# Cosine attention and an MLP mixer on one core: w1 fetched early, the copies of w2 spread over three slot ends, and two pieces of the start moved to GpSimd

## Chip, core and metric

One core of a Trainium2 chip. The metric is the device time of the program in microseconds (us), median of several runs. The kernel before takes 393.95 us. All runs whose state is recorded were in the fast state; the mean clock granted to the tensor engine differs from run to run (0.985 to 1.0).

## The reference, cut to what matters

```python
# q, k, v: (8 batches, 12 heads, 448 rows, 64), float32
q_n = q / (norm(q) + 1e-6);  k_n = k / (norm(k) + 1e-6)
attn = softmax(q_n @ k_n.T / tau)
x = (attn @ v) in the shape (8, 448, 768)
u = x + (relu(x.T @ w_tok1) @ w_tok2).T      # token mixing
out = u + relu(u @ w_ch1) @ w_ch2            # channel mixing
```

## The kernel before

The kernel works on 48 pairs of heads, one pair in each "slot" of a software pipeline. The 448 rows of a head are 3 x 128 "main" rows and 64 "X" rows. For each pair: squares and sums of q and k, their norms, scaled q and k, a transpose, scores, exponentials, and the product with v; then token mixing (w1 is w_tok1, w2 is w_tok2) two or three slots later and, from slot 6 on, channel mixing, which fills the tensor engine. In these traces every engine runs its instructions in the order in which the program gives them. So an instruction that waits holds back all that stand behind it on its engine: in the changed kernel the sums of pair 2 wait 2.66 us for GpSimd, and the copy behind them waits as long; a run below puts that copy ahead of the sums, and it comes sooner.

The start, before slot 0, and the ends of the first slots are what the change touches:

```python
    def weights_tok():
        nc.gpsimd.dma_start(out=w1t[:, 0:NC, :], ...)       # main part of w1
        nc.gpsimd.dma_start(out=w1t[0:XR, NC, :], ...)      # its X rows
        nc.gpsimd.dma_start(out=w2n[0][:], ...)             # w2, still in its natural order

    def place_w2():                                         # w2 into the order that the matmul reads
        nc.vector.tensor_copy(out=w2t[:, :, XR:S]..., in_=w2n[0][:, :, 0:SM]...)
        nc.vector.tensor_copy(out=w2t[:, :, S:S + XR], in_=w2n[0][:, :, SM:S])

    def place_w2_odd():                                     # the X columns once more, for odd batches
        nc.vector.tensor_copy(out=w2t[:, :, 0:XR], in_=w2n[0][:, :, SM:S])
    # ...
        squares_x(0, nc.scalar, nc.gpsimd)
        rnorms(0, 21, 33)
        scaled(1, nc.gpsimd)
        # ...
        score_main0(0, 2)
        squares(2, nc.scalar, nc.gpsimd)
        score_main0(1)
        scaled_x(0, nc.vector, 0, 1)          # pair 0's X rows
        scaled_x(0, nc.gpsimd, 1, HP)         # those of pairs 1 and 2
        sums(2)                               # vector engine
        score_main0(2)
        tpose_x(0, pst)
        for lo, n in ((P * NC, P), (P * 7, XR)):
            nc.vector.tensor_copy(out=qks[0][:, lo:lo + n], in_=pst[:, lo:lo + n])
        rnorms(0, 33, 45)
        score_rest0()
        score_x(0)
        weights_tok()
        cast_vx(0)
        cast_v(0)                             # vector engine
        scaled(2, nc.gpsimd)
        for i in range(NP_ALL + 2):           # the slots
            # ... pair 3's squares in slot 0, q and k both on the scalar engine
            if i == 2:
                place_w2()
            if i == 3:
                place_w2_odd()
```

Of the kernel before, what the change touches and what calls it, by code (L numbers as in the profile page):

```python
# [22 lines left out]
def kernel(  # L23
# [12 lines left out]
    nc = tc.nc  # L36

    B, H, S, E = q.shape
# [5 lines left out]
    NC = 3  # L44
# [45 lines left out]
    w2n = []  # L90
# [46 lines left out]
    def mh(at, p):  # L137
        return at[p // HP][:, 2 * (p % HP):2 * (p % HP) + 2]

    def weights_tok():  # L140
        nc.gpsimd.dma_start(out=w1t[:, 0:NC, :], in_=moe_w_tok1[0:SM].rearrange("(p c) t -> p c t", c=NC))
        nc.gpsimd.dma_start(out=w1t[0:XR, NC, :], in_=moe_w_tok1[SM:S])
        w2n.append(mix.tile([P, TT, S], FP16, name="w2n", tag="gt16", bufs=1))
        nc.gpsimd.dma_start(out=w2n[0][:], in_=moe_w_tok2.rearrange("(tt p) s -> p tt s", p=P))

    def place_w2():
        nc.vector.tensor_copy(out=w2t[:, :, XR:S].rearrange("t a (c p) -> t a c p", c=NC),
                              in_=w2n[0][:, :, 0:SM].rearrange("t a (p c) -> t a c p", c=NC))
        nc.vector.tensor_copy(out=w2t[:, :, S:S + XR], in_=w2n[0][:, :, SM:S])  # L149

    def place_w2_odd():
        nc.vector.tensor_copy(out=w2t[:, :, 0:XR], in_=w2n[0][:, :, SM:S])

    def weights_ch1(i):
        n = C // 2
# [31 lines left out]
    def squares_x(n, eq, ek):  # L187
        square(eq, sqx[0:XR, 0:6], xh(xq, n, 6))
        square(ek, sqx[:, 6:9], xh(xk, n, HP))
# [257 lines left out]
    def at(slots):  # L447
        got = {}
        for p, s in slots.items():
            got.setdefault(s, []).append(p)  # L450
        return got


    FIRST = NPAIR
    early_sq = {3: 0, 4: 1, 5: 1, 6: 3, 7: 4, 8: 5, 9: 5, 10: 6, 11: 7, 12: 8, 13: 9, 14: 9, 15: 10, 16: 11, 17: 11}
    sq_slot = {p: early_sq.get(p, p - 6) for p in range(3, NP_ALL)}
    sq_at = at(sq_slot)
    sum_at = at({p: s + 1 for p, s in sq_slot.items() if p < 8 or p >= 18})

    rn_at = {}  # L460
    for n in range(1, NHALF):
        for c0, c1 in ((0, 21), (21, 45)) if n < 4 else ((0, 45),):
            s = 1 + sq_slot[3 * n + (0 if c1 == 21 else 2)]
            rn_at.setdefault(s, []).append((n, c0, c1))
    sc_at = at({p: {7: 6}.get(p, p - 2 if p < DMA_FROM else p - 3) for p in range(3, NP_ALL)})
    early_qk = {2: 0, 3: 4, 4: 6, 5: 7}
# [30 lines left out]
    def norm_begin(p, eq, ek):  # L497
        squares(p, eq, ek)
        if p % HP == 0:
            squares_x(p // HP, eq, ek)  # L500
# [11 lines left out]
    with tc.manual_schedule():  # L512
# [53 lines left out]
        tpose_main(0, pst, 0)  # L566
        tpose_main(0, pst, 1)
        squares_x(0, nc.scalar, nc.gpsimd)
        rnorms(0, 21, 33)
        scaled(1, nc.gpsimd)  # L570
        nc.scalar.copy(out=qks[0][:, 0:SM], in_=pst[:, 0:SM])
# [1 line left out]
        nc.vector.tensor_copy(out=qks[0][:, 512:512 + SM], in_=pst[:, 512:512 + SM])  # L573
        rnorms(0, 0, 9)
        busy(w, 2)
        score_main0(0, 2)
        squares(2, nc.scalar, nc.gpsimd)
        score_main0(1)
        scaled_x(0, nc.vector, 0, 1)
        scaled_x(0, nc.gpsimd, 1, HP)  # L580
        sums(2)
        score_main0(2)
# [3 lines left out]
        rnorms(0, 33, 45)  # L586
        score_rest0()
        score_x(0)
        weights_tok()
        cast_vx(0)  # L590
        cast_v(0)
        scaled(2, nc.gpsimd)
        for i in range(NP_ALL + 2):
            if i < DMA_FROM:
                loads(i)
            if DMA_FROM <= i + 2 < NP_ALL:
                dma_tpose(i + 2)
            if i - 2 in X_DMA:
                x_tpose(i - 2)
            for p in ut_at.get(i, ()):  # L600
                u_tpose(p)
            if i >= DMA_FROM:
                loads(i)

            left = next((t + 1 - i for t in sorted(tok2_at) if t >= i + (i == FIRST) and
                         any(p % NPAIR == NPAIR - 1 for p in tok2_at[t])), 6)
            if FIRST <= i < 2 * NPAIR:
                quota = max(len(queue) - 6, 0) * ns(S, DT) / (2 * NPAIR - i)
            else:
                quota = max(sum(t for t, _ in queue) - 2000.0, 0.0) / left  # L610
            def next_qk(p):
                if p < min(DMA_FROM, NP_ALL):
                    qk_copy(p, tpose(p))

            def tok2(p):
                m_tok2(p)
                if p % NPAIR == NPAIR - 1:
                    queue.extend(ch_units(p // NPAIR))

            def norm_rn():  # L620
                for n, c0, c1 in rn_at.get(i, ()):
                    rnorms(n, c0, c1)

            def next_sq(ps):
                for p in ps:
                    norm_begin(p, nc.scalar if p < 18 else nc.gpsimd, nc.scalar if p == 3 else nc.vector if p in (10, 11, 12, 15) else nc.gpsimd)

            if i == FIRST:
                next_sq([9])
                rnorms(2, 21, 33)  # L630
                norm_scale(7, nc.gpsimd)
                pv(i - 1)
                m_tok1(i - 2)
                tok2(i - 3)
                next_qk(i)
                tok2(i - 2)
                m_tok1(i - 1)
                score(i, 0)
                score(i, 1)
                score(i, 2)  # L640
                tok2(i - 1)
                norm_sums(8)
                norm_sums(9)
            elif 0 < i < NP_ALL:
                score(i, 0, 2 if i < 4 else 0)
                score(i, 1)
                score(i, 2)
            for p in sum_at.get(i, ()):
                norm_sums(p)
            if i < FIRST:  # L650
                norm_rn()

            if i < FIRST:
                next_sq([p for p in sq_at.get(i, ()) if p != 9])
                for p in sc_at.get(i, ()):
                    norm_scale(p, nc.gpsimd)
            def casts():
                for n in castx_at.get(i, ()):
                    cast_vx(n)
                for n in cast_at.get(i, ()):  # L660
                    cast_v(n)
                if i in (2, 5):
                    weights_ch1(i // 4)
                if i in (7, 8):
                    weights_ch2(i - 7)

            if i <= FIRST:
                casts()

            if i < FIRST:  # L670
                for p in tok2_at.get(i, ()):
                    tok2(p)
                if i == 3:
                    next_qk(i + 1)
                if i:
                    pv(i - 1)
                if i:
                    score_x(i)
                if i in (0, 1, 2, 4):
                    next_qk(i + 1)  # L680
                for p in tok_at.get(i, ()):
                    m_tok1(p)
            elif i == FIRST:
                feed(0.0, 1000.0)
                score_x(i)
                feed(0.0, 1000.0)
                rnorms(2, 33, 45)
                norm_scale(8, nc.gpsimd)
                rnorms(3, 0, 21)
                next_qk(i + 1)  # L690
                next_sq(sq_at[i])
                norm_sums(10)
                feed(0.0, 1000.0)
            else:
                def norm_next():
                    norm_rn()
                    for p in sc_at.get(i, ()):
                        norm_scale(p, nc.gpsimd)

                if i >= 2 * NPAIR:  # L700
                    next_sq(sq_at.get(i, ()))
                if i < DMA_FROM:
                    norm_next()
                    casts()
                fed[0] = 0.0
                feed(quota * 0.3, 900.0 if i < DMA_FROM else 1800.0)
                if i < NP_ALL:
                    score_x(i)
                if i >= DMA_FROM:
                    norm_next()  # L710
                    casts()
                next_qk(i + 1)
                if i <= NP_ALL:
                    pv(i - 1)
                both = [p for p in tok2_at.get(i, ()) if p in tok_at.get(i, ())]
                if not both:
                    feed(quota * 0.3)
                for p in tok_at.get(i, ()):
                    m_tok1(p)
                if i < 2 * NPAIR:  # L720
                    next_sq(sq_at[i])
                if both:
                    feed(quota * 0.3, 900.0)
                for p in tok2_at.get(i, ()):
                    tok2(p)
                if i < 2 * NPAIR:
                    for p in sq_at[i]:
                        norm_sums(p)
                feed(quota * 0.4, 900.0 if i >= 2 * NPAIR else 0.0)
            if i == 2:  # L730
                place_w2()
            if i == 3:
                place_w2_odd()
        for p in ut_at.get(NP_ALL + 2, ()):
            u_tpose(p)
        feed(1e9)
# [35 lines left out]
```

## Time and profile before

| | kernel before |
|---|---|
| time, median (range) | 393.95 us (393.75 to 393.95) |
| span in the profile | 391.6 us |
| tensor engine busy | 378.7 us |
| first exponential of slot 7 (a slot starts with its pair's first exponential) | 50.56 us |
| from there to the end | 391.61 - 50.56 = 341.05 us |

In the lists in order of time the columns are: start in us, busy us, engine, source line and operation, output and inputs, shapes, count; in brackets the engine's idle time just ahead, and what ended it. PE is the tensor engine, ACT the scalar engine, DVE the vector engine, POOL GpSimd. Source lines are those of each kernel's own text: the changed kernel's are 3 or 4 higher up to the start-up part (its L214 is the L211 of before, L305 the L302, L250 the L247).

Two lengths are used below to compare profiles. The first is the time from the first exponential of all (10.44 us here) to the first exponential of slot 7, with the slots between. The second is what remains after it. I worked both lengths out from the starts of the rows of the exponentials; each profile is of one run, and that of the kernel before is of a run of 393.38 us, shorter than any of the five behind the median.

### The profile page before, as it was taken

The numbers are of one execution on the slowest core, as the hardware profiler recorded it, in microseconds if no ns is written. First come the engines' busy times: TensorE is split into PE (matmuls) and PEld (weight loads), VectorE is DVE, ScalarE is ACT, GpSimd is POOL, SyncE is SP. The second block draws the span as 40 slices with busy tenths as digits, with TensorE's granted clock in tenths as the row PEclk, the third lists the DMA queues.
The fourth block names the chain that finished last, engine by engine and source line by source line (L and its number), as shares of the span: only waits on it lengthen the run. The fifth ranks groups of instructions, "written<-read, shape, count | busy, mean of one in ns | idle before, by whom it ended". The sixth has DMA issues, their size and how long they took to land.

```text
span 391.6 us, 9075 instructions
## 1 busy us (share of the span) xinstructions
PE 378.7 (97%) x3658; PEld 228.9 (58%) x3658; DVE 193.6 (49%) x368; ACT 226.1 (58%) x411; POOL 209.6 (54%) x306
## 2 busy tenths in 40 slices
PE   7678999999999999999999999999999999999996
PEld 2356655665565656565566565565566566565554
DVE  5688758866244654446534545346434342333022
ACT  5998698843765548673775546673765535511400
POOL 4978486589476675768673938658551700000000
PEclk9699999999999999999999999999999999999999
DMA  8999989988988988999999899799982453023013
GB/s 204 267 242 221 256 238 187 201 213 241 208 170 200 211 166 194 222 166 223 199 239 174 177 253 206 155 192 175 244 142 55 133 114 69 16 60 102 3 40 121
DMA packets 137514, 67.51 MB, mean 172 GB/s; under 512 B 93248, under 2 KB 134016, under 8 KB 137472
## 3 DMA queue, kind: packets, MB, share of 16 engines
q1 hardware_dynamic: 133296, 61.36, 72.0%
q0 software_dynamic: 3632, 5.18, 7.7%
q8 instruction: 28, 0.46, 0.5%
q10 hardware_dynamic: 544, 0.39, 0.3%
q14 instruction: 14, 0.11, 0.1%
HBM read 43.38 MB, written 11.01 MB: 139 GB/s over the span
## 4 chain that ended last, share of the span: by engine, by line
PE 88%; ACT 7%; DVE 3%; DMA 1%; issue 1%; SPq 0%; DVEq 0%
PE psF L404 28%; PE psG L389 28%; PE psO L320 9%; PE psS L301 7%; PE psR L341 5%; PE psU L361 4%; ACT pt L302 3%; PE psO L322 3%; PE psX L308 2%; DMA qm<-in_q_dram 1%; PE psU L366 1%; ACT sq L178 1%; PE pst L243 1%; ACT pt L309 1%; ACT rn L203 1%
## 5 line engine op out<-in xcount | busy, mean ns | idle before, releaser
L302 ACT ACTIVATE pt<-psS 128x896 f16<-128x896 f32 x141 | 119.1, 921 | 64.6 <-PE psS L301 64.3
L389 PE MATMUL psG<-ut,wc1t 128*128 128x448 f16 x576 | 119.5, 353 | 0.2
L404 PE MATMUL psF<-wc2t,gt 128*128 128x384 f16 (+2 forms) x684 | 117.3, 323 | 0.1
L391 ACT ACTIVATE gt<-psG 128x448 f16<-128x448 f32 x96 | 51.1, 557 | 71.9 <-PE psG L389 71.9
L404 PEld LDWEIGHTS <-gt 128*128 128x128 f16 x684 | 64.5, 98 | 47.1 <-issue 6.8
L389 PEld LDWEIGHTS <-wc1t 128*128 128x128 f16 x576 | 53.2, 98 | 52.4 <-issue 8.7
L211 POOL TENSOR_TENSOR kq<-km,rn 128x384 f16<-128x384 f32 x47 | 39.4, 838 | 77.4 <-ACT rn L204 77.2
L407 DVE TENSOR_TENSOR ost<-psF,ur 128x384 f32<-128x384 f32 (+2 forms) x57 | 31.4, 550 | 87.2 <-PE psF L404 87.2
L320 PEld LDWEIGHTS <-pt 128*128 128x128 f16 x1152 | 50.8, 98 | 8.5 <-issue 2.4
L320 PE MATMUL psO<-vt,pt 128*128 128x65 f16 x1152 | 53.1, 194 | 1.1 <-ACT pt L302 0.8
L326 DVE RECIPROCAL rec<-psO 128x8 f32<-128x8 f32 x48 | 9.9, 207 | 81.5 <-PE psO L322 81.5
L193 DVE TENSOR_REDUCE ssq<-sq 128x12 f32<-128x768 f32 (+1 forms) x49 | 45.1, 929 | 6.0 <-ACT sq L178 3.1
L180 POOL TENSOR_TENSOR sq<-km 128x384 f32<-128x384 f32 x42 | 34.4, 822 | 15.1 <-DMA km<-in_k_dram 14.8
L322 PE MATMUL psO<-vx,pt 128*128 128x130 f16 x192 | 42.1, 219 | 0.0
L211 POOL TENSOR_TENSOR kq<-qm,rn 128x384 f16<-128x384 f32 x47 | 39.6, 842 | 0.0
L301 PE MATMUL psS<-qk 64*128 64x448 f16 x282 | 36.2, 357 | 1.3 <-DVE qk L261 0.9
L327 DVE TENSOR_TENSOR x<-psO,rec 128x512 f16<-128x512 f32 x48 | 33.2, 691 | 1.7
L341 PE MATMUL psR<-x,w1t 128*128 128x128 f16 x384 | 29.2, 219 | 0.1
L309 ACT ACTIVATE pt<-psX 128x448 f16<-128x448 f32 x48 | 27.1, 564 | 3.3 <-PE psX L308 2.3
L361 PE MATMUL psU<-w2t,r 128*128 128x448 f16 x96 | 25.9, 353 | 1.5 <-DVE w2t L149 1.1
L180 POOL TENSOR_TENSOR sq<-qm 128x384 f32<-128x384 f32 x30 | 24.7, 823 | 1.1 <-DVE ssq L193 0.3
L341 PEld LDWEIGHTS <-w1t 128*128 128x128 f16 x384 | 23.8, 97 | 2.1 <-issue 0.4
(76 smaller groups left out, 320.4 us busy)
## 6 DMA issues: line engine op xcount, KB each, us to landing
vm<-in_v_dram SPq DMA_DIRECT2D x16, 576.0 KB, 5.3
out_dram<-ost SPq DMA_DIRECT2D x23, 384.0 KB, 2.9
qm<-in_q_dram SPq DMA_DIRECT2D x14, 576.0 KB, 5.2
km<-in_k_dram SPq DMA_DIRECT2D x14, 576.0 KB, 5.2
wc1t<-in_moe_w_ch_dram POOLq DMA_DIRECT2D x2, 1152.0 KB, 13.9
wc2t<-in_moe_w_ch_dram POOLq DMA_DIRECT2D x2, 1152.0 KB, 12.9
out_dram<-ost SPq DMA_DIRECT2D x9, 192.0 KB, 2.7
xq<-in_q_dram SPq DMA_DIRECT2D x7, 192.0 KB, 5.1
```

Of the source, the lines that this page charges most:

```text
L180: eng.tensor_tensor(out=out, in0=src, in1=src, op=ALU.mult)
L193: nc.vector.tensor_reduce(out=ssqs[p // HP % 3][:, lo + 6 * a0:lo + 6 * a1], in_=sq[p][:, a0:a1].rearrange("p a g e -> p (a g) e"), axis=A ...
L211: eng.tensor_tensor(out=kqs[n % 2][:, j, a, 0:NC, :].rearrange("p c (g e) -> p g c e", g=2), in0=src, in1=_bcast_free(rn, E), op=ALU.mult)
L301: nc.tensor.matmul(psS[:, g, 0:S], qk[r, P * c:P * (c + 1)], qk[r, 512:512 + S], start=True, stop=True)
L302: nc.scalar.activation(out=pt[:, 2 * S * c:2 * S * (c + 1)].rearrange("p (g s) -> p g s", g=2), in_=psS[:, :, 0:S], func=AF.Exp, scale=inv ...
L320: nc.tensor.matmul(psO[:, m, E1 * g:E1 * (g + 1)], pt[:, at:at + P], vt[:, 2 * j + g, c, 0:E1], start=(g == 0 and c == 0), stop=False)
L322: nc.tensor.matmul(psO[:, m, 0:2 * E1], pt[:, PX + P * m:PX + P * (m + 1)], vx[:, j, 0:2 * E1], start=False, stop=True)
L341: nc.tensor.matmul(psR[:, tt, :], w1t[:, m, tt * P:(tt + 1) * P], xs[p][:, m, :], start=(m == 0), stop=(m == NC))
L361: nc.tensor.matmul(psU, rs[p][:, tt, :], w2t[:, tt, lo:lo + S], start=(tt == 0), stop=by_dma and tt == TT - 1)
L389: nc.tensor.matmul(psG[:], wc1t[:, dt, ct * P:(ct + 1) * P], ut[:, dt, sp], start=(dt == 0), stop=(dt == DT - 1))
L391: nc.scalar.activation(out=gt[:, ct, sp], in_=psG[:], func=AF.Relu)
L404: nc.tensor.matmul(psF[:, 0:w], gt[:, ct, lo:lo + P], wc2t[:, ct, P * i0:P * i1], start=(ct == 0), stop=(ct == CT - 1))
```

## The change

Four parts. (1) Pair 0's X rows are scaled on GpSimd, ahead of pair 2's squares, and not on the vector engine. (2) Pair 3's k squares go from the scalar engine to GpSimd, and the instructions of all its squares move from slot 0 to just before it. (3) The three copies of w2 are spread over the ends of slots 1, 2 and 3. (4) The main part of w1 is fetched some 5 us earlier, in a stretch where GpSimd idles, and w2 before the X rows of w1.

```diff
+    def weights_tok1(x):          # the X rows of w1 if x, else the main part
+    def weights_tok2():           # w2
+    def place_w2_x(lo):
+        nc.vector.tensor_copy(out=w2t[:, :, lo:lo + XR], in_=w2n[0][:, :, SM:S])
 ...
         squares_x(0, nc.scalar, nc.gpsimd)
+        weights_tok1(0)
         rnorms(0, 21, 33)
 ...
+        scaled_x(0, nc.gpsimd, 0, 1)
         score_main0(0, 2)
         squares(2, nc.scalar, nc.gpsimd)
         score_main0(1)
-        scaled_x(0, nc.vector, 0, 1)
         scaled_x(0, nc.gpsimd, 1, HP)
 ...
-        weights_tok()
+        weights_tok2()
+        weights_tok1(1)
         cast_vx(0)
         cast_v(0)
+        squares_x(1, nc.scalar, nc.gpsimd)
+        squares(3, nc.scalar, nc.gpsimd)
         scaled(2, nc.gpsimd)
 ...
+            if i == 1:
+                place_w2()                # now the main copy alone
             if i == 2:
-                place_w2()
+                place_w2_x(S)
             if i == 3:
-                place_w2_odd()
+                place_w2_x(0)
```

More of the change, by code (lines that the diff above doesn't have):

```diff
@@ L138, in mh @@
         return at[p // HP][:, 2 * (p % HP):2 * (p % HP) + 2]
-    def weights_tok():
-        nc.gpsimd.dma_start(out=w1t[:, 0:NC, :], in_=moe_w_tok1[0:SM].rearrange("(p c) t -> p c t", c=NC))
-        nc.gpsimd.dma_start(out=w1t[0:XR, NC, :], in_=moe_w_tok1[SM:S])
+    def weights_tok1(x):
+        if x:
+            nc.gpsimd.dma_start(out=w1t[0:XR, NC, :], in_=moe_w_tok1[SM:S])
+        else:
+            nc.gpsimd.dma_start(out=w1t[:, 0:NC, :], in_=moe_w_tok1[0:SM].rearrange("(p c) t -> p c t", c=NC))
+    def weights_tok2():
         w2n.append(mix.tile([P, TT, S], FP16, name="w2n", tag="gt16", bufs=1))
@@ L148, in place_w2 @@
                               in_=w2n[0][:, :, 0:SM].rearrange("t a (p c) -> t a c p", c=NC))
-        nc.vector.tensor_copy(out=w2t[:, :, S:S + XR], in_=w2n[0][:, :, SM:S])
-    def place_w2_odd():
-        nc.vector.tensor_copy(out=w2t[:, :, 0:XR], in_=w2n[0][:, :, SM:S])
+    def place_w2_x(lo):
+        nc.vector.tensor_copy(out=w2t[:, :, lo:lo + XR], in_=w2n[0][:, :, SM:S])
     def weights_ch1(i):
@@ L454 @@
     FIRST = NPAIR
-    early_sq = {3: 0, 4: 1, 5: 1, 6: 3, 7: 4, 8: 5, 9: 5, 10: 6, 11: 7, 12: 8, 13: 9, 14: 9, 15: 10, 16: 11, 17: 11}
-    sq_slot = {p: early_sq.get(p, p - 6) for p in range(3, NP_ALL)}
+    early_sq = {4: 1, 5: 1, 6: 3, 7: 4, 8: 5, 9: 5, 10: 6, 11: 7, 12: 8, 13: 9, 14: 9, 15: 10, 16: 11, 17: 11}
+    sq_slot = {p: early_sq.get(p, p - 6) for p in range(4, NP_ALL)}
     sq_at = at(sq_slot)
-    sum_at = at({p: s + 1 for p, s in sq_slot.items() if p < 8 or p >= 18})
+    sum_at = at({p: s + 1 for p, s in ({3: 0} | sq_slot).items() if p < 8 or p >= 18})
     rn_at = {}
@@ L462 @@
         for c0, c1 in ((0, 21), (21, 45)) if n < 4 else ((0, 45),):
-            s = 1 + sq_slot[3 * n + (0 if c1 == 21 else 2)]
+            s = 1 + ({3: 0} | sq_slot)[3 * n + (0 if c1 == 21 else 2)]
             rn_at.setdefault(s, []).append((n, c0, c1))
@@ L625, in next_sq @@
                 for p in ps:
-                    norm_begin(p, nc.scalar if p < 18 else nc.gpsimd, nc.scalar if p == 3 else nc.vector if p in (10, 11, 12, 15) else nc.gpsimd)
+                    norm_begin(p, nc.scalar if p < 18 else nc.gpsimd, nc.vector if p in (10, 11, 12, 15) else nc.gpsimd)
             if i == FIRST:
```

## The prediction

> **What bounds the kernel now.** I read the page first, then the busy time in short windows, then the start-up in order of time, engine by engine, then the chain of waits for the same stretch. The page gives the frame:
>
> ```profile
> span 391.6 us, 9075 instructions
> PE 378.7 (97%) x3658; PEld 228.9 (58%) x3658; DVE 193.6 (49%) x368; ACT 226.1 (58%) x411; POOL 209.6 (54%) x306
> PE   7678999999999999999999999999999999999996
> ```
>
> The tensor engine is busy 97% of the span, and its row falls under 9 only in the first four slices of 9.8 us and the last. The change touches nothing after slot 3 (some 35 us), and the comparison of the instruction streams shows no tensor instruction added, removed or reordered. So all it can do is shift the moment at which the full tensor stream begins; the idle tensor time of the whole kernel is 391.6 - 378.7 = 12.9 us, and only what lies between 10 and 35 us is within reach. The windows:
>
> ```profile
> 10.00:15.00 5.00, 2.36 (x22) 1.37 (x21) 3.63 (x7) 4.52 (x13) 4.92 (x8) 0.76 0.94 273
> 15.00:20.00 5.00, 4.73 (x47) 2.67 (x45) 2.53 (x5) 4.93 (x11) 3.95 (x7) 0.56 1.17 271
> 25.00:30.00 5.00, 3.86 (x56) 2.45 (x54) 4.58 (x8) 3.99 (x8) 4.47 (x6) 1.00 1.04 216
> ```
>
> (PE, PEld, DVE, ACT, POOL, granted clock, DMA share, GB/s.) At 10 to 20 us the scalar engine and GpSimd are nearly full; at 25 to 30 us the vector engine is. The waits that the change aims at, from the tensor engine's own list in order of time:
>
> ```profile
> 12.43 0.23 PE L247 MATMUL pst<-id,kq 128*128 128x128 f16 x1 [1.82 <-DVE kq L222]
> 13.64 0.34 PE L288 MATMUL psS_r<-qk 64*128 64x64 f16 x6 [0.82 <-DVE qk L585]
> 27.44 0.54 PE L361 MATMUL psU<-w2t,r 128*128 128x448 f16 x2 [1.14 <-DVE w2t L149]
> ```
>
> The first is pair 0's X rows scaled on the vector engine, the third the copy of w2 into its place. What the vector engine, the scalar engine and GpSimd do there:
>
> ```profile
> 10.57 0.89 DVE L217 TENSOR_TENSOR kq<-xq,rn 64x128 f16<-64x128 f32 x1 [0.67 <-ACT rn L204]
> 11.38 0.99 DVE L222 TENSOR_TENSOR kq<-xk,rn 64x64 f16<-64x64 f32 x2
> 12.40 0.95 DVE L193 TENSOR_REDUCE ssq<-sq 128x12 f32<-128x768 f32 x1
> 25.56 1.09 DVE L147 COPY w2t<-w2n 128x768 f16<-128x768 f16 x1
> 26.57 0.81 DVE L149 COPY w2t<-w2n 128x128 f16<-128x128 f16 x1
> ```
>
> ```profile
> 15.69 0.53 ACT L178 ACTIVATE sq<-km 128x384 f32<-128x384 f32 x1
> 16.52 0.36 ACT L178 ACTIVATE sqx<-xk 128x192 f32<-128x192 f32 x1
> 16.88 2.54 ACT L302 ACTIVATE pt<-psS 128x896 f16<-128x896 f32 x3
> 19.29 0.32 ACT L201 ACTIVATE rn<-ssq,tiny 128x21 f32<-128x21 f32 x1
> ```
>
> ```profile
> 10.49 0.83 POOL L180 TENSOR_TENSOR sq<-km 128x384 f32<-128x384 f32 x1
> 11.27 0.66 POOL L217 TENSOR_TENSOR kq<-xq,rn 64x256 f16<-64x256 f32 x1
> 16.76 0.82 POOL L211 TENSOR_TENSOR kq<-qm,rn 128x384 f16<-128x384 f32 x1
> 20.55 0.83 POOL L211 TENSOR_TENSOR kq<-km,rn 128x384 f16<-128x384 f32 x1 [1.40 <-ACT rn L204]
> 26.19 1.14 POOL L211 TENSOR_TENSOR kq<-qm,rn 128x384 f16<-128x384 f32 x1
> ```
>
> **What the Trainium skill says.** Page "SBUF — State Buffer", section "Who interferes with whom": a vector instruction with two SBUF inputs, or a copy in a two-port mode, and a GpSimd instruction that reads SBUF hold one port pair as an exclusive lock, and the second to start blocks; a reduction does not contend. The trace agrees: the vector engine's 64x128 multiply took 0.89 us beside a GpSimd multiply that ended at 11.31, while its own 128x384 ones took 0.55 alone; the w2 copy took 1.09 with GpSimd busy until 26.2, and the GpSimd multiply behind it 1.14 in place of 0.82. Page "DMA: Bandwidth & Descriptors", section "SWDGE vs HWDGE vs iDMA": transfers that GpSimd issues have their descriptors written by GpSimd itself. The trace has 0.74, 0.92 and 0.73 us of GpSimd time for the three token-weight transfers. Page "TensorE: Matmul & The Clock Gate", Part 1: the clock is decided in free-running windows of about 3.4 us. The trace grants half clock from about 12.8 to 19.6 us, two such windows, after the 1.82 us idle; whether a different idle pattern changes that no run here shows.
>
> **The change part by part.** Times are estimates carried forward from the rows above.
>
> Part 1, pair 0's X rows on GpSimd. The vector engine loses 0.89 + 0.99 us. GpSimd's forms of 64x256 and 64x384 took 0.66 and 0.82, so 64x128 is about 0.50; its pairs of 64x128 took 0.39 each and 64x192 0.50, so 64x64 is about 0.29 each plus 0.08 between. Start at 10.55 (the norm is ready at 10.53): done at about 11.7 in place of 12.37. The transposes come 0.65 us sooner. But pair 2's k squares now start at 11.7 and end at 12.5, and the sums of pair 2, next in the vector engine's order and ahead of the copy that the transposes feed, start at 12.53 in place of 12.40. The copy, the rest of the scores and the norm behind them move by +0.13, not by -0.65. Gain: none.
>
> Part 2, pair 3's k squares on GpSimd. The scalar engine sheds the two rows of k; at their spacing, 0.41 + 0.36 = 0.77 us. But the exponential at 16.88 began as the tensor engine's scores came (16.86), so it cannot start sooner; with part 1 it is at about 17.0. GpSimd gains 0.47 + 0.79 us of spacing plus part 1's 1.2 us, less the w1 issue of 0.74 that moves into its idle stretch at 7.5. Its stream after the X rows: scaled pair 2 ends at about 19.3 (before 17.6), pair 3's k squares at 17.75 (the scalar engine had them at 16.9). The sums of pair 3 and its X rows (0.95 + 0.74) then end at 19.4, just when the three exponentials are done (19.5). Scaled pair 3 begins behind the squares of pairs 4 and 5 at 20.9, not 20.55. Gain: none; loss about 0.35 on GpSimd, mostly hidden.
>
> Part 3, w2 copied a slot earlier. The main copy lands at 21.3, between pair 2's copy and the sums of pairs 4 and 5. It meets GpSimd's scaling of pair 3, waits for the lock to about 21.7 and ends by 22.2; GpSimd pays another 0.3 to 0.4. So pair 3's X rows end at about 24.7, before 24.0, its transpose waits from 24.3 to 24.7, and its copy and scores come about 0.5 to 0.6 late. In slot 3 only the small copy is left ahead of the token matmul: it ends near 26.5 in place of 27.4, and the tensor engine, done with its scores at 26.85, does not wait. The 1.14 us wait is gone, and 0.6 of it is spent on the late scores.
>
> Part 4, w1 early. The DMA queues are full (share 0.9 to 1.2) except at 9 to 10.5 us, so the transfer fills a gap and then delays v of pair 0 (landed 13.14, needed at 13.5) by up to about 1 us; the cast has until 15.5, when pair 1's copy needs the vector engine. w2 no longer queues behind w1: it landed 7.2 us after its issue, and now should land near 20, ahead of 21.3. w1 itself was never waited for. Gain: none directly.
>
> Sum: about +0.13 at the first scores, +0.15 at slot 2, +0.6 at slot 3's scores, then -1.0 from the w2 wait: slot 4 begins about 0.36 us earlier. From there every row shifts alike. 393.95 - 0.36 = 393.6; I take 393.5, as the estimates for GpSimd's collisions lean to the heavy side.
>
> **The rivals.** First: GpSimd becomes the bound of slots 1 to 3. For it: it has 4.92 of 5 us busy at 10 to 15, and takes on about 1.7 us more there net. Against it: it idles 1.40, 1.41 and 1.66 us before the scalings of pairs 3, 4 and 6. If each of those delays reaches the tensor engine, the time is 394.2 to 394.6. Second: w2 lands after 21.3 and blocks the in-order vector engine ahead of pair 4's sums and pair 1's division. For it: the earlier landing time 21.56. Against: less ahead of it in its queue. That would cost 0.5 to 1 us at slot 2 and eat the gain: 394.0 to 394.5. Third: the shorter idle keeps the full clock through 13 to 19 us, so that the scalar engine's 0.77 us count and the second slot starts sooner: at most 0.8 us more, 392.7. Against: pair 3's sums at 19.4 then hold the norm anyway.
>
> **Range and chances.** The third rival sets the low end, 392.6, the first two the high end, 394.4. Two per cent is 7.9 us of the 12.9 us of idle tensor time, most of it untouched, so faster has 0.005, slower 0.005, same 0.99.
>
> **What would show it.** In the profile after: the X transpose of pair 0 near 11.8 instead of 12.43, and the copy behind it still waited for, until about 13.7; the first exponential of slot 1 near 17.0 with scalar idle time ahead of it; pair 3's scaling on GpSimd starting near 20.9 with no wait; the transpose of pair 3's X rows waiting for GpSimd; no wait for w2; the exponentials of slot 4 near 30.65 instead of 31.01. The prediction is wrong if the wait for the sums of pair 2 doesn't hold back the copy, if slot 3's scores are not late, or if the full clock is granted between 13 and 19 us.

## The result, and the profile after

| | before | changed |
|---|---|---|
| median (range), first chip, 5 runs each | 393.95 (393.75 to 393.95) | 393.34 (392.66 to 393.65) |
| ratio there, with 95% interval | | 0.9984 (0.997 to 0.9999) |
| median, another chip (11 and 5 runs) | 393.80 | 393.68 |
| ratio there | | 1.0001 (0.9988 to 1.0014) |
| span in the profile | 391.6 | 391.7 |

A ratio is the mean time of one kernel's fast runs over that of the other's of the same rounds, so it is not quite the ratio of the medians quoted. The two medians say 0.61 and 0.12 us less; the two intervals together reach from 0.30% less to 0.14% more: within 2% by far.

The tensor engine's own rows in order of time, changed kernel:

```profile
11.68 0.23 PE L250 MATMUL pst<-id,kq 128*128 128x128 f16 x1 [1.06 <-POOL kq L225]
13.80 0.34 PE L291 MATMUL psS_r<-qk 64*128 64x64 f16 x6 [1.76 <-DVE qk L589]
26.65 0.55 PE L364 MATMUL psU<-w2t,r 128*128 128x448 f16 x2
27.95 0.34 PE L246 MATMUL pst<-id,kq 128*128 128x128 f16 x3 [0.38 <-POOL kq L214]
35.14 0.74 PE L304 MATMUL psS<-qk 64*128 64x448 f16 x6 [0.92 <-DVE qk L264]
```

Both waits that the change aimed at are shorter or gone: X transposes at 11.68 instead of 12.43, and the token matmul no longer waits for w2. But the next wait took over each time. The scores behind the X transposes start at 13.80 instead of 13.64, since their copy stands behind the sums of pair 2. And the scores of slot 5 wait 0.92 us for the vector engine. Its rows:

```profile
12.56 0.95 DVE L196 TENSOR_REDUCE ssq<-sq 128x12 f32<-128x768 f32 x1 [2.66 <-POOL sq L183]
15.03 0.76 DVE L169 CAST vt<-vm 128x1152 f16<-128x1152 f32 x1 [1.29 <-DMA vm<-in_v_dram]
21.38 0.75 DVE L151 COPY w2t<-w2n 128x768 f16<-128x768 f16 x1
26.00 0.53 DVE L155 COPY w2t<-w2n 128x128 f16<-128x128 f16 x1
30.79 0.84 DVE L155 COPY w2t<-w2n 128x128 f16<-128x128 f16 x1
```

The sums of pair 2 wait for GpSimd's squares (2.66 us). The cast of v, which waited for nothing before, now waits 1.29 us for v to land. The same 128x128 copy takes 0.53 and 0.84 us. On GpSimd:

```profile
20.88 0.82 POOL L214 TENSOR_TENSOR kq<-km,rn 128x384 f16<-128x384 f32 x1
21.67 1.14 POOL L214 TENSOR_TENSOR kq<-qm,rn 128x384 f16<-128x384 f32 x1
26.45 1.45 POOL L214 TENSOR_TENSOR kq<-qm,rn 128x384 f16<-128x384 f32 x1
30.75 0.82 POOL L214 TENSOR_TENSOR kq<-km,rn 128x384 f16<-128x384 f32 x1
```

The multiply that takes 0.82 alone takes 1.14 where it meets the main copy of w2, and 1.45 where it meets the small copy and the cast of v. The last row is the one that the 0.84 us copy ran into: it started 0.04 us ahead of the copy and ended at 31.57, and the copy ended at 31.63. The exponentials of slots 1, 3, 4 and 5:

```profile
17.04 2.54 ACT L305 ACTIVATE pt<-psS 128x896 f16<-128x896 f32 x3 [0.68 <-PE psS L304]
26.38 2.54 ACT L305 ACTIVATE pt<-psS 128x896 f16<-128x896 f32 x3 [0.44 <-PE psS L304]
30.79 2.54 ACT L305 ACTIVATE pt<-psS 128x896 f16<-128x896 f32 x3 [0.45 <-PE psS L304]
35.54 2.54 ACT L305 ACTIVATE pt<-psS 128x896 f16<-128x896 f32 x3 [0.33 <-PE psS L304]
```

and, for comparison, rows of the kernel before from the same lists (scalar engine, vector engine, GpSimd) that the prediction did not show:

```profile
31.01 2.54 ACT L302 ACTIVATE pt<-psS 128x896 f16<-128x896 f32 x3 [0.45 <-PE psS L301]
35.41 2.54 ACT L302 ACTIVATE pt<-psS 128x896 f16<-128x896 f32 x3
```

```profile
31.00 0.49 DVE L152 COPY w2t<-w2n 128x128 f16<-128x128 f16 x1
```

```profile
30.62 0.82 POOL L211 TENSOR_TENSOR kq<-km,rn 128x384 f16<-128x384 f32 x1
```

Slot 4 starts at 30.79 instead of 31.01: a lead of 0.22 us. Slot 5 starts at 35.54 instead of 35.41: the lead is gone and 0.13 us more. In both kernels the odd copy (the third copy of w2, for odd batches) ends 0.05 to 0.06 us after GpSimd's multiply does (31.44 to 31.49, 31.57 to 31.63). Being ready earlier doesn't help the vector engine there; it only waits longer. And GpSimd is 0.13 us later in the changed kernel.

### The profile page after: what moved, and what is told of

The parts are those of the page before. It is cut to its first block, busy times and chain, and to the rows that moved or that the text cites. A ratio compares the mean times of both kernels' runs of the same rounds, so it can differ in the third digit from the quotient of the medians.

```text
span 391.7 us, 9074 instructions
## 1 busy us (share of the span) xinstructions
PE 379.2 (97%) x3658; PEld 229.3 (59%) x3658; DVE 191.8 (49%) x365; ACT 225.4 (58%) x409; POOL 211.9 (54%) x311
## 4 chain that ended last, share of the span: by engine, by line
PE 88%; POOL 3%; ACT 3%; DVE 2%; issue 2%; DMA 1%; SPq 1%; POOLq 0%
PE psF L407 28%; PE psG L392 28%; PE psO L323 9%; PE psS L304 7%; PE psR L344 5%; PE psU L364 4%; PE psO L325 3%; PE psX L311 2%; ACT pt L305 2%; POOL kq L214 1%; DMA xk<-in_k_dram 1%; PE pst L246 1%; PE psU L369 1%; POOL sq L183 1%; POOL kq L225 0%
## 5 line engine op out<-in xcount | busy, mean ns | idle before, releaser
L183 POOL TENSOR_TENSOR sq<-km 128x384 f32<-128x384 f32 x43 | 35.3, 823 | 12.8 <-DMA km<-in_k_dram 12.6
L183 POOL TENSOR_TENSOR sq<-qm 128x384 f32<-128x384 f32 x30 | 24.7, 822 | 1.7 <-DMA qm<-in_q_dram 0.9
```

Source lines behind the costliest of these rows:

```text
L183: eng.tensor_tensor(out=out, in0=src, in1=src, op=ALU.mult)
```

## The experiments

Theory A is what the trace after suggested: the change gains a little up to slot 4 and gives it back in slot 5 through the odd copy, so that it is worth next to nothing at like clock. The rivals are named in each expectation. "Like clock" matters because the changed kernel's first five runs were 393.52 and 393.65 at a mean clock of 0.991, and 393.18, 393.34 and 392.66 at 0.996.

All profiles together. The columns are: mean of the runs minus the mean of the kernel before on the same chip in the same rounds; start of slots 1, 3, 4, 5 and 7, counted from the first exponential of all; the length of slot 4 (slot 5 less slot 4); landing of v of pair 0 (from the run's start).

| kernel | mean time, difference | slot 1 | slot 3 | slot 4 | slot 5 | slot 7 | slot 4 long | v lands |
|---|---|---|---|---|---|---|---|---|
| before | | 6.44 | 15.37 | 20.57 | 24.97 | 40.12 | 4.40 | 13.14 |
| before, again | -0.10 | 6.45 | 15.32 | 20.51 | 24.91 | 40.06 | 4.40 | 13.00 |
| changed | -0.62 | 6.60 | 15.94 | 20.34 | 25.10 | 40.25 | 4.76 | 15.01 |
| changed, again | -0.01 | 6.60 | 15.80 | 20.39 | 25.15 | 40.30 | 4.76 | 14.57 |
| changed, odd copy late | -0.66 | 6.60 | 15.77 | 19.98 | 24.30 | 39.44 | 4.32 | 13.92 |
| before, odd copy late | +0.05 | 6.36 | 15.23 | 20.43 | 24.76 | 39.89 | 4.33 | 13.68 |
| before, w2 copies alone | +0.12 | 6.36 | 16.43 | 21.05 | 25.80 | 40.95 | 4.75 | 13.12 |
| changed, k squares back | -0.50 | 6.59 | 15.76 | 20.29 | 25.04 | 40.18 | 4.75 | 14.79 |
| changed, X copy first | -0.49 | 5.97 | 15.64 | 19.97 | 24.72 | 39.87 | 4.75 | 14.85 |
| odd copy late, w1 late | -0.54 | 6.59 | 16.20 | 20.42 | 24.74 | 39.88 | 4.32 | 13.18 |
| odd copy late, X copy first | -0.25 | 7.27 | 16.88 | 21.60 | 25.92 | 41.06 | 4.32 | 15.77 |
| the same, k squares back | -0.52 | 6.14 | 15.31 | 19.89 | 24.21 | 39.35 | 4.32 | 14.54 |
| before, dummy matmuls | +0.37 | 6.33 | 15.18 | 20.38 | 24.78 | 39.92 | 4.40 | 12.71 |
| changed, dummy matmuls | +0.09 | 6.74 | 17.26 | 21.48 | 25.89 | 41.04 | 4.41 | 15.38 |

Single runs of the kernel before scatter by 0.33 us (standard deviation of 28 runs at a clock of 0.991), so a difference of means of five runs under 0.3 us says little by itself. The column of slot 7 scatters no less: in 13 of the 14 profiled runs the time is the start of slot 7, from the run's start, plus 342.81 to 342.83 us, so what makes one run longer than another lies before slot 7. The two profiles of the kernel before agree within 0.06 us, but they are of runs of 393.38 and 393.42 us, and none is of a run near 394. So differences of slot 7 of some 0.2 us between single profiles show little; the length of one slot, and the rows that set it, show more. The table's differences are over all listed runs; the ratios below are as recorded, and in the dummy matmuls, with runs far apart, the two don't have the same sign.

**The kernel before again** (no edit).

> The kernel before, unchanged, as a control: does it too have runs with a mean granted clock of 0.996 beside 0.991, and are those shorter? Theory A (the change is worth next to nothing where the clock is alike; the 0.6 us come from runs with one half-clock window instead of two, which the new order makes likelier): runs at 0.996 appear here too and are 0.3 to 0.9 us shorter than those at 0.991, or never appear and the time stays 393.75 to 393.95. Theory B (the change saves about 0.5 us in every run): all runs 393.75 to 393.95 whatever the clock, span 391.6.

Measured: 393.5 us median, ratio 0.9997 (0.9985 to 1.0009). Runs at 0.996 appear here too. 38 runs of the kernel before have their clock recorded: 28 at 0.991 with a mean of 393.86, 10 at 0.995 or 0.996 with 393.52. So in the kernel before more clock goes with 0.34 us less (0.13 to 0.46 on the three chips). It doesn't in every kernel: with w1 late (below) the three runs at 0.995 or 0.996 averaged 393.32, the two at 0.991 393.18. The ten runs of the changed kernel on two chips: five at 0.991 with a mean of 393.72, five at 0.995 or 0.996 with 393.30, 0.15 and 0.22 us under the kernel before at like clock. The clocks of the five runs of before on the first chip weren't recorded, so how much of the first 0.6 us was clock stays open. Theory B, 0.5 us in every run, is hard to hold.

**The changed kernel again** (no edit).

> The changed kernel again, for a second profile and runs on the chip of the others. Everything after the first exponential of slot 7 has lasted 341.04 us in every profile so far that kept its clock, so the kernels are compared by that moment, counted from the first exponential of all: 40.12 and 40.06 in the two profiles of the kernel before, 40.25 in the one of the changed kernel, 39.44 with the late odd copy. Theory A (net nothing: the lead of slot 4 is given back in slot 5 by the odd copy): 40.1 to 40.3 again with two half-clock windows; time within 0.3 of the kernel before at like clock. Theory B (0.5 us saved): 39.5 to 39.7.

Measured: 393.68 us median, ratio 1.0001 (0.9988 to 1.0014), slot 7 at 40.30 against 40.25 in the first profile. Theory A's figures, not B's.

**The odd copy late.**

```diff
-            if i == 3:
+            if i == 5:
                 place_w2_x(0)
```

> The changed kernel with the second small copy of w2 (0.84 us on the vector engine at 30.79, beside GpSimd's scaling) moved from the end of slot 3 to the end of slot 5. Theory A says that this copy gives the 0.22 us lead of slot 4 back in slot 5: here the scores of slot 5 start by 34.9 instead of 35.14 and the first exponential of slot 7 near 50.2 to 50.4 instead of 50.69, and the time is 0.3 to 0.4 us under the changed kernel's at the same clock. Theory B: no difference beyond 0.1, as another wait takes its place.

```profile
26.51 1.43 DVE L169 CAST vt<-vm 128x1152 f16<-128x1152 f32 x1
30.31 0.95 DVE L196 TENSOR_REDUCE ssq<-sq 128x12 f32<-128x768 f32 x1
38.54 0.18 DVE L155 COPY w2t<-w2n 128x128 f16<-128x128 f16 x1
```

```profile
26.49 0.83 POOL L214 TENSOR_TENSOR kq<-qm,rn 128x384 f16<-128x384 f32 x1
```

(Vector engine and GpSimd, in order of time.) The copy now meets only the last 0.10 us of a square on GpSimd (37.81 to 38.64) and takes 0.18 us, and the sums that stood behind it at 31.55 start at 30.31. Slot 7 comes at 39.44 (50.09 from the run's start), and the time is 393.16 us median, ratio 0.9983 (0.9971 to 0.9995). The length of slot 4 is what tells: 4.32 here against 4.76. In the table it is 4.75 or 4.76 in five of the six profiles of kernels that spread the copies of w2 and keep the odd one in slot 3 (the exception, 4.41, is the one with dummy matmuls: there the copy began 0.37 us ahead of slot 4, in the five together with it), and 4.32 or 4.33 in all five with it late. So theory A's wait is shown: the odd copy in slot 3 costs the changed kernel 0.44 us (0.43 in the pair of kernels with the X copy first, which differ in this move alone). The rest of the 0.81 us to the changed kernel was there by slot 4 (19.98 against 20.34), ahead of the move, and the rows tell most of it. In the changed kernel the cast of v in slot 3 went ahead of GpSimd's multiply:

```profile
26.46 0.75 DVE L169 CAST vt<-vm 128x1152 f16<-128x1152 f32 x1
```

The cast took 0.75 us, the multiply 1.45, and pair 4's transposes waited for it. In this run the multiply went first (0.83 us), the cast took 1.43, and the transposes didn't wait. From slot 3 to slot 4 it is 4.21 or 4.22 us in the three profiles where the multiply took 0.83 (this one, w1 late, and the changed kernel with dummy matmuls), and 4.33 to 4.72 in the seven of spread copies where it took 1.44 or 1.45. In the first two of the three as in the seven the two rows start 0.01 us apart, the multiply's first, so the rows don't tell which will win, and no edit aimed at it. That part of this run's lead, 0.19 us to the first profile of the changed kernel and 0.38 to the second, is not a gain of the move.

**The kernel before with the odd copy late** (the same edit on the kernel before).

> The kernel before with its second X copy of w2 moved from the end of slot 3 to the end of slot 5, nothing else. It tells how much of the gain of the late odd copy belongs to the change. Counted from the first exponential of all, slot 7 came at 40.06 to 40.12 before, 40.25 and 40.30 changed, 39.44 changed with the late copy. Theory A (the change leads by 0.2 at slot 4 whatever the copy does, and the copy takes 0.35 to 0.4 out of slot 4 in the changed kernel, some 0.4 also here): 39.65 to 39.8 here, so that the changed kernel with the late copy leads by 0.2 to 0.35. Rival D (in the kernel before the copy was hidden, at 0.49 us): no change here, 40.0 to 40.1, and all of the 0.65 us belongs to the change plus the move.

Measured: slot 4 is 4.33 long instead of 4.40 and slot 7 comes at 39.89; 393.7 us median, ratio 1.0003 (0.999 to 1.0016). So in the kernel before the copy cost 0.07 us only, less than theory A's 0.4. It was nearly hidden there, as rival D said, though slot 7 lies between the two. The 0.44 us is then a cost of the change itself. In the changed kernel the vector engine waits in slot 3 for pair 4's transposes, which wait for GpSimd:

```profile
28.52 0.66 DVE L264 COPY qk<-pst 128x960 f16<-128x960 f16 x1 [0.45 <-PE pst L251]
```

From there it runs at a fixed distance behind GpSimd: in all five profiles with this wait and the copy in slot 3 (the next run is one of them), the copy starts 0.03 to 0.04 us after GpSimd's multiply and takes 0.83 or 0.84 us. In the three profiles of the kernel before with the copy in slot 3 there is no such wait, the copy starts 0.38 to 0.39 us after the multiply, and it takes 0.48 or 0.49.

**The copies of w2 alone, on the kernel before** (part 3 without the others).

```diff
             if i == 1:
+                place_w2()                # main copy alone
             if i == 2:
-                place_w2()
+                place_w2_x(S)
             if i == 3:
-                place_w2_odd()
+                place_w2_x(0)
```

> The kernel before with the earlier copies of w2 alone. Theory A: this part carries all of the gain: slot 4 at 20.0 to 20.2 from the first exponential (20.57 before, 20.34 changed), as the losses of parts 1 and 2 are absent; slot 7 at 39.5 to 39.9, and if the odd copy meets GpSimd's lock in slot 4 up to 0.35 later. Rival B (the four parts need each other: without the earlier w2 transfer the copy waits for its landing at 21.6 to 22.4 and holds up the vector engine): slot 3 at 15.9 or later, slot 4 no earlier than 20.5.

```profile
22.36 1.04 DVE L147 COPY w2t<-w2n 128x768 f16<-128x768 f16 x1 [1.79 <-DMA w2n<-in_moe_w_tok_dram]
```

Theory A fell here and rival B held: w2 landed at 22.34, the vector engine stood 1.79 us for it, slot 3 came at 16.43 and slot 7 at 40.95, later than in the kernel before. The time, 394.12 us median, ratio 1.0004 (0.9988 to 1.0019), doesn't show it, with one run at 392.25. In the changed kernel w2 landed at 20.69, ahead of its copy at 21.38. So part 3 needs the earlier w2 of part 4 (no run has part 4 alone). The early w1 isn't what it needs: with w1 fetched late but w2 issued first (below), w2 landed at 21.23, ahead of its copy at 21.55.

**Pair 3's k squares back on the scalar engine** (part 2 undone as to the engine).

```diff
-        squares_x(1, nc.scalar, nc.gpsimd)
-        squares(3, nc.scalar, nc.gpsimd)
+        squares(3, nc.scalar, nc.scalar)
+        squares_x(1, nc.scalar, nc.scalar)
```

> The changed kernel with pair 3's k squares back on the scalar engine. Theory A (part 2 gains nothing, as the scalar engine waits for the scores at 17.0, and costs GpSimd 1.3 us): pair 3's scaling on GpSimd starts at 20.6 instead of 20.88, slot 3 at 15.6 to 15.8 instead of 15.94, slot 7 at 40.0 to 40.15, so the same or 0.1 to 0.25 better. Rival B (part 2 is a gain): slot 1 and slot 7 0.3 or more later.

```profile
20.58 0.83 POOL L214 TENSOR_TENSOR kq<-km,rn 128x384 f16<-128x384 f32 x1 [1.06 <-ACT rn L207]
```

GpSimd starts pair 3's scaling at 20.58 and has idled 1.06 us by then, where it had no idle time in the changed kernel. Slot 1 is not later (6.59), slot 7 at 40.18, 393.31 us median, ratio 0.9988 (0.9976 to 1.0). Part 2 gains nothing: the scalar engine has the room, as it waits for the scores of slot 1 anyway. By slot 7 this run is 0.07 and 0.12 us ahead of the two profiles of the changed kernel, too little to call a cost. Its five runs, all at 0.991, average 0.49 us less than the changed kernel's on the same chip; the profile doesn't show that much, and the cause stays open.

**Pair 0's X copy ahead of the sums of pair 2.**

```diff
-        sums(2)
         score_main0(2)
         tpose_x(0, pst)
         for lo, n in ((P * NC, P), (P * 7, XR)):
             nc.vector.tensor_copy(...)
-        rnorms(0, 33, 45)
+        sums(2)
         score_rest0()
         score_x(0)
+        rnorms(0, 33, 45)
```

> The changed kernel with the copy of pair 0's X transposes ahead of the sums of pair 2, and the norm behind the X scores, so that what part 1 gains is not held by that wait. Theory A: the X scores of pair 0 start near 12.7 instead of 14.08, so the order held them; but slot 1 stays at 6.4 to 6.6 from the first exponential, as v of pair 0 lands at 15.0 behind w1 and its cast holds pair 1's copy, and slot 7 stays at 40.0 to 40.3. Rival B (that wait was all that kept part 1 from paying): slot 1 earlier by 0.6, slot 7 by 0.4 or more.

```profile
13.08 0.26 PE L291 MATMUL psS_r<-qk 64*128 64x64 f16 x6 [0.42 <-DVE qk L588]
```

This run's first exponential came at 11.06 us, 0.3 to 0.7 later than in the others, so in relative terms the scores behind the X copy start 2.02 us after it, against 13.80 - 10.44 = 3.36 in the changed kernel: the order had held them. Slot 1 comes at 5.97 and slot 7 at 39.87, 0.4 sooner, 393.23 us median, ratio 0.9988 (0.9976 to 1.0). These are rival B's figures, not theory A's. With the start of this run late by that much, v was less late relative to it (14.85, as in the changed kernel, but against a later start), so one profile can't say how much of the 0.4 us the reordering would give with a usual start.

**Both moves together.** The odd copy late and the X copy first (no further edit).

> The changed kernel with the late odd copy and with pair 0's X copy ahead of the sums of pair 2. If the two gains add (0.83 and 0.4 us by the moment of slot 7): 39.0 to 39.1 and 392.5 to 392.8. If GpSimd's scaling of pair 3 holds slot 3 in both: 39.3 to 39.45, nothing more than the late copy.

```profile
15.79 0.76 DVE L169 CAST vt<-vm 128x1152 f16<-128x1152 f32 x1 [2.21 <-DMA vm<-in_v_dram]
```

A miss: slot 7 at 41.06, 393.53 us median (392.93 to 394.38), ratio 0.9995 (0.9983 to 1.0007). The profiled run was the slowest of its six, at a clock of 0.985. v landed at 15.77, its cast waited 2.21 us, pair 1's copy stands behind the cast, and slot 1 came at 7.27. So v, pushed back by w1, is the next wait, and it is not a steady one: 13.92 to 15.77 in the eight profiles with w1 early, 12.71 to 13.68 in the six with it late.

**The same with pair 3's k squares back** (the edit of part 2 undone, added).

> The one before it, with pair 3's k squares back on the scalar engine. With slot 1 no longer held by the copy, the scalar engine's 0.77 us may now count: slot 1 0.3 to 0.7 later than there; but GpSimd is 1.3 us ahead, so slot 3 is 0.1 to 0.3 earlier. Slot 7 between 38.9 and 39.2; if it is above the one before by 0.2 or more, part 2 pays once part 1 is let through.

Measured: slot 1 at 6.14, slot 7 at 39.35, a span of 390.8 us, the shortest profile of all; 393.09 us median (392.59 to 394.9), ratio 0.9992 (0.9975 to 1.0009). Slot 7 lies above the range expected and below the kernel before it, whose run had v 1.2 us later, so the comparison that I meant to make isn't settled.

**w1 fetched late again** (the odd copy late, and part 4's first half undone).

```diff
-        weights_tok1(0)
         rnorms(0, 21, 33)
 ...
         weights_tok2()
+        weights_tok1(0)
         weights_tok1(1)
```

> The changed kernel with the late odd copy, and the large part of w1 fetched after w2 again. Theory A: v of pair 0 lands by 13.3 and its cast waits for nothing, but the issue's 0.74 us goes back into GpSimd's busy stretch and its chain up to pair 3's X rows runs 0.4 to 0.7 later: slot 7 at 39.7 to 40.1 against 39.44. Rival E (the late v is the larger cost): slot 7 at 39.4 or earlier.

Measured: v landed at 13.18 and its cast did not wait; pair 3's scaling on GpSimd began at 21.20 instead of 20.88; slot 7 came at 39.88 against 39.44. That is theory A's figure. But the time is 393.2 us median, all five runs within 393.16 to 393.42, ratio 0.9988 (0.9976 to 1.0). The means differ by 0.11 us from the early w1's (across two chips) and the spread is the smallest of the experiments. The early w1 buys GpSimd some room and pays with an unsteady v.

**Dummy matmuls, changed kernel**, to keep the clock full where the tensor engine idles from 10.6 to 13.8 us.

```diff
         score_main0(2)
+        busy(w, 4)
         tpose_x(0, pst)
+        busy(w, 7)
```

> The changed kernel with 4 and 7 dummy matmuls in the idle tensor time between 10.6 and 13.8 us, so that the clock stays full. Theory A: the clock is 1.0 from 12.8 on, the first exponential of slot 1 starts at 16.3 to 16.4 instead of 17.04, and if the clock is what tells the changed kernel's runs apart, all runs are at 393.2 or below. Rival C (the clock does not matter, since the sums of pair 3 at 19.4 and GpSimd's scaling hold slot 2 anyway): the norm of slot 1 still starts at 19.4 to 19.5, slot 3's exponentials still at 26.3 to 26.4, and the time stays at 393.3 to 393.6.

```profile
16.79 0.74 PE L304 MATMUL psS<-qk 64*128 64x448 f16 x6 [1.36 <-DVE qk L264]
```

Neither theory: with a full clock at 15 us the scores of slot 1 still started at 16.79, behind a wait of 1.36 us, since the cast of v waited for its landing at 15.38 and pair 1's copy stood behind the cast. The tensor engine, busy for 2.90 of the 5 us from 15 to 20, then got half clock from 23.1 to 26.5 us in this run. Six runs: 392.47, 392.74 and 393.18 at a clock of 1.0, 393.97 at 0.999, and 395.39 and 395.62 at 0.993; ratio 0.9993 (0.9972 to 1.0015). The three at 1.0 average 392.80, 1.0 us under the kernel before; but the kernel before with a full clock (next) shows no gain, so that the clock is worth this is not shown. Of the 395.62 of the profiled run, 1.30 us lie in the last output writes.

**Dummy matmuls, kernel before** (8 ahead of the X transposes, 3 after).

> The kernel before with 8 and 3 dummy matmuls in the same place, full clock. The scalar engine reached the first exponential of slot 1 at 16.87 just as the scores came at 16.86, so with a full clock it still starts at 16.9. Theory A: about 393.6 to 393.9, near the kernel before. Theory B: the same. If it falls to 393.2 or below, the clock alone is worth as much as the whole change.

Measured: clock full in the profiled run, slot 1 at 6.33, slot 7 at 39.92, 393.78 us median (393.13 to 395.86), ratio 1.0009 (0.999 to 1.0028). Slot 1 gains 0.11 us and slot 7 0.2; three of six runs had a clock of 1.0 and took 393.13, 394.94 and 393.63, 393.90 on average. So the clock alone is not worth the change's first 0.6 us.

**A version that beats both?** By mean time the changed kernel with the odd copy late is the best (0.66 us, 0.17%, under the kernel before in the same rounds). The interval of its ratio, 0.9971 to 0.9995, lies below 1, but overlaps those of all the others, and part of the lead of its profile was the order of the cast and the multiply. Of the moves tried on top of the change, the late odd copy alone has a cost shown that it removes (0.44 us of slot 4); on the kernel before it gains 0.07 us.

## Why the prediction was right or wrong

The time, 393.34 us, is 0.16 us under the 393.5 predicted. The range held the median on both chips. That the number is so near is luck, as the last points show. Step by step:

- Part 1. Right: the transposes came at 11.68 (11.7 predicted), the sums of pair 2 at 12.56 (12.53), the scores behind the copy 0.16 late (0.13). The reordered run shows that the order was what held them.
- Part 2. Right: the exponentials of slot 1 at 17.04 (17.0) after 0.68 us of scalar idle time, pair 3's scaling at 20.88 (20.9). Undoing it cost nothing.
- Part 3 up to slot 3. Right: pair 3's X transposes came at 24.70 (24.7), slot 3's scores 0.57 late (0.6), the small copy ended at 26.53 (26.5), and the token matmul didn't wait. The new wait, 0.38 us of pair 4's transposes for GpSimd, wasn't foreseen: its multiply took 1.45 us and not the 0.8 that I let it have, as it was blocked by the small copy and by the cast of v. With it slot 4 led by 0.22 us, not 0.36; in the second pair of profiles by 0.12. The 0.1 us taken off because the collisions were judged too heavy went the wrong way.
- Part 4. "Gain: none directly" is not tested alone, but it undersells: the copies of w2 alone lose, as w2 then lands at 22.34. v was delayed by 1.9 us in the profile, not 1; the margin (15.5) was passed by 0.2 there and by more in others.
- "From there every row shifts alike" is the step that failed. I left out the third copy, the odd one in slot 3: it became 0.84 us, where it had been 0.49, and slot 4 was 0.36 us longer (4.76 against 4.40). By slot 7 the two profiles of the changed kernel are 0.18 us later than the two of before (40.25 and 40.30 against 40.12 and 40.06), where I had -0.36.
- The rivals. GpSimd did become the bound, not by its load but by the lock, and in slots 3 and 4. w2 wasn't late in the changed kernel, but is where it isn't fetched earlier. The full clock was not granted between 13 and 19 us in either profile (the half clock of the kernel before lasted from 12.6 to 19.4 us, not from 12.8 to 19.6 as the prediction reads it); where dummies forced it, v was the wait that took its place.

What stays open: the runs say -0.62 and -0.01 us, the profiles +0.18 by slot 7. The two don't contradict each other: the profiled runs themselves took 393.38 and 393.42 us before, 393.52 and 393.68 changed. The scatter of single runs is as large as these, each profile is of one run, and the clocks of the first chip's runs of before are missing. So the right total doesn't come from the mechanism, of which the profiles show no gain left by slot 7; that the change is worth less than 0.3% is all that is shown.

## What to carry to other kernels

When a vector copy and a GpSimd multiply can meet, what the copy costs depends on where in the multiply it arrives: the same 128x128 copy took 0.18, 0.49 and 0.84 us, and moving other work earlier changed which. Place such small copies where GpSimd idles, and look at them again after each shift. Where an instruction of each engine starts within 0.01 us of the other's, look at several profiles: either went first here, and a multiply took 0.83 or 1.45 us by it. A wait removed from an in-order engine pays only if nothing that stands between it and its user has a later wait of its own; and a transfer started early can take its time from others (v landed later here), so look up which of them had no margin.

## What the Trainium skill lacked or had wrong

- Page "SBUF — State Buffer", section "Who interferes with whom": the exclusive lock agrees with the rows shown. For the vector engine blocked by GpSimd the page has a factor from one measurement (6.8 times slower) and no time for the handover. Here the odd copy in slot 3 ended 0.05 to 0.06 us after GpSimd's multiply (31.44 to 31.49, 31.57 to 31.63). The page says that the order of issue decides who blocks; it has nothing on near ties, where rows 0.01 us apart went both ways (multiply 1.44 or 1.45 us in seven profiles, 0.83 in two).
- Page "DMA: Bandwidth & Descriptors", section "SWDGE vs HWDGE vs iDMA": it says that the two kinds of transfer take turns on the engines. It has no figure for what an early GpSimd-issued load does to plain loads in flight: v landed at 13.92 to 15.77 us with w1 early and at 12.71 to 13.68 with it late.
- Page "TensorE: Matmul & The Clock Gate", Part 1: windows of 3.4 us agree (half clock lasted 3.4 or 6.8 us in most profiles). Its section "Terms" puts the penalty at the throttled time times one less the clock ratio, which for one window of 3.4 us is an estimate of 1.7 us; it has no word on stretches where the tensor engine waits for others. Here the runs of before at a mean clock of 0.995 or 0.996 were 0.34 us shorter than those at 0.991.
